# Input sums begun in the chunk's own step, and all four sums of a forward unit at the step's head: one change to a fused spectral mixing and MLP kernel

## The chip, the cores and the metric

The kernel runs on one NeuronCore of a Trainium2 chip. Its time is the device time of one execution in microseconds (us). Five engines work side by side, each through its own queue in order: TensorE (PE in the profile; PEld is its weight loading), VectorE (DVE), ScalarE (ACT), GpSimd (POOL) and SyncE (SP, which here only issues transfers). Transfers are also issued from GpSimd's queue. Sixteen DMA engines carry all of them.

## The reference

```python
def _attn_ref(x, filt_r, filt_i):            # x: (8, 3008, 256), filters: (1505, 256)
    X = np.fft.rfft(x, axis=1)
    F = (filt_r + 1j * filt_i)[None, :, :]
    return np.fft.irfft(X * F, n=x.shape[1], axis=1).astype(np.float32)

def _moe_ref(x, w_in, w_out):                # x: (24064, 256), w_in: (256, 2048), w_out: (2048, 256)
    h = x @ w_in
    relu6 = np.clip(h + 3.0, 0.0, 6.0)
    g = h * relu6 / 6.0
    return (g @ w_out).astype(np.float32)

# reference: _moe_ref(_attn_ref(x, filt_r, filt_i).reshape(24064, 256), w_in, w_out)
```

A sequence is filtered in frequency, and every token then passes an MLP with the activation hard-swish. All is float32.

## The kernel before, in words

**The MLP** works in 47 blocks k of 512 tokens (256 pairs), each in 8 parts p of 256 hidden columns. One (k, p) is a *step*; a plain step takes 6.08 us. "12.3" below is step 3 of block 12. Both products are done by a Strassen scheme with seven products of half size instead of eight. In a step TensorE does seven up products of block k (`up_1` to `up_5`) and seven down products of the step before (`down`), woven together. ScalarE copies partial results (L990, L991, L1000, L1019) and computes the inner part of the activation (L1024). VectorE adds (L1005, L1010), finishes the activation (L1029, in `hswish`) and makes the sums that the down products need (L1036, L1037 in `g_sums`, L1042 in `g_last`). `hswish(1)` and `g_sums` of a step are issued at the beginning of the next one, and its second down product needs them.

**The input sums** of a block, `xt`, are five combinations of the four parts of the block's spectral result (`xn`, a ring of three blocks). They are needed from the next block's first step on (`up_1`). They are made in one of two ways when `ready(i)` finds that chunk i completes a block. For most blocks ScalarE makes five copies (`t_copy`, L956), and three calls of `t_add` (L961) issue transfers from GpSimd's queue that add other parts in place: the first adds to four of the five sums, the second to four beginning with another one, the third is two transfers, of which one adds the tile `minus`. Because they add to the same places, each waits for the landing of the one before. For the other blocks `t_sums` lets GpSimd compute them (L970).

**The spectral part** for the later batches is spread over the MLP's steps. A table `plan` holds for each step five *places* with calls. In a step with a unit the order is: place 3, the activation's rest and `g_sums`, `g_last` unless the step counts as late, place 4, first down products, `up_1`, place 0, more down products, `up_2`, L1005, L1010 and the rest, place 1 (behind `up_4` and the first L1024), `up_5`, the last down products, place 2. Each engine gets its instructions in this order. A step i counts as late (`late`) in steps 1 and 2 of a block, and when places 0 to 2 of step i-1 hold one of the heavy VectorE functions, `a8_sums` among them; then `g_last` follows L1010 instead of `g_sums`.

From batch 2 on the work of batch n follows a cycle of six blocks, named in `kinds` by the letters "caxFFF". The first three (c, a, x) do the forward transform of four chunks c = 0 to 3, and the three F blocks the rest of it, the filter and the inverse transform. A *forward unit* is:

- `a8_unit` (L609, place 3): 32 small matmuls into four PSUM banks, two of which ScalarE copies (L613);
- `a8_sums(n, c, r)` for r = 0 and 1 (L619, L620): a sum and a difference of a copied and a PSUM half, in VectorE;
- `a8_folds(n, c, par)` (L627), two calls one step apart: they write two tiles `y`, of which there are only two buffers;
- `z8_store` (L648 to L654): the tiles go to DRAM, half of the stores from GpSimd's queue and half from SyncE's.

In groups n = 3 to 7 the units stand at steps c.3, a.2, x.2 and x.5, the folds of chunk 2 at x.3 and x.4, its store at the end of x.4, the first fold of chunk 3 at the end of x.5, and its store at the end of x.6. For n = 2 chunk 0 and 1 stand a little later (c.5, a.3). `t2_load` reads the stored values back at the end of block x, for F.2.

The chunk that completes a block does so in step 1 of the block before the one that uses the sums; 30 of these blocks (the a, x and F blocks of six groups) take the way by copies and transfers.

Of the kernel before, what the change touches and what calls it, by code (L numbers as in the profile page):

```python
# [229 lines left out]
def kernel(  # L230
# [585 lines left out]
    for b in range(B):  # L816
# [4 lines left out]
        n = 0  # L821
# [12 lines left out]
    def pair(i):  # L834
        b, js, o, n = chunks[i]
        return b * HC * NA + o, n
# [39 lines left out]
    def ready(i):  # L876
        t, n = pair(i)
        k = t // PAIRS
        if (t + n) // PAIRS > k > 0:
            if n_at[i] % NP == 1 and k - 1 in kinds:  # L880
                st["xt", k] = xtp.tile([P, 5, PAIRS], FP32, name="xt")
                for j, (step, place_) in enumerate(((1, 1), (2, 0), (2, 1), (2, 1), (3, 0), (3, 1), (3, 2), (4, 1))):
                    plan.setdefault((n_at[i] + step, place_), []).append((t_copy if j < 5 else t_add, (k, j % 5)))
            else:
                t_sums(k)


    def n_five(i, ends_step=False):
        b, js, o, n = chunks[i]
        s0 = i % 2 * NJ  # L890
        banks = [psU.tile([P, 512], FP32, name=x) for x in ("al", "be")] if ends_step else [
            psF.tile([P, 512], FP32, name="psn", tag="f") for c in range(2)]
        ps = [t[:, 0:2 * n].rearrange("p (e n) -> p e n", e=2) for t in banks]
        for q, j in enumerate(js):
            for dh in range(2):
                for g in range(2):
                    for c in range(2):
                        r = ds(c * HALF, ATOM)
                        nc.tensor.matmul(ps[c][ts(g, HALF), dh, ts(q, NA)], t4[r, s0 + q, ds(dh * P + g * HALF, HALF)],  # L899
                                         groups[r, j, :], start=True, stop=True)  # L900
        for c in range(2):
            ring(i, 0, n, o, lambda at_: xn[:, :, c, at_], ps[c])
        ready(i)

    def n_unit(i, dh):
        if spare[i]:
            ps = st["po", n_at[i] // NP][2][:, 1, :, :].rearrange("p u m -> p (u m)") if dh else st["al"][:, 256:512]
        else:
            ps = psF.tile([P, 512], FP32, name="psn", tag="f")
        b, js, o, n = chunks[i]  # L910
        for q, j in enumerate(js):
            w = edges[0:2 * ATOM, FIRST.index(j), :] if i >= TAIL and j else ones[0:2 * ATOM, j, :]
            strips(ps[:, ts(q, TOK)], t4[0:2 * ATOM, i % 2 * NJ + q, ts(dh, P)], w, start=not spare[i], stop=True)
        for q, a, m, to in TO.get(i, [(q, 0, NA, o + q * NA) for q in range(len(js))]):
            ring(i, a, m, to, lambda at_: xn[:, dh, :, at_], ps[:, ts(q, TOK)].rearrange("p (c n) -> p c n", c=2))
        if dh:
            ready(i)
# [45 lines left out]
    def t_sums(k):  # L963
        t = xtp.tile([P, 5, PAIRS], FP32, name="xt")
        c0, s0, c1, s1 = (xb(k, d, c) for d in range(2) for c in range(2))
        u, v = (t[:, i, :] for i in (F5, F3))
        f1, f2, f3, f4, f5 = (t[:, i, :] for i in (F1, F2, F3, F4, F5))
        for o, x0, x1, op_ in ((f1, c0, s0, ALU.subtract), (u, c0, c1, ALU.add), (v, s0, s1, ALU.add),
                               (f4, u, v, ALU.subtract), (f5, u, v, ALU.add), (f2, c1, s1, ALU.add), (f3, f1, f2, ALU.add)):
            nc.gpsimd.tensor_tensor(out=o, in0=x0, in1=x1, op=op_)  # L970
        st["xt", k] = t
# [211 lines left out]
    plan = {}  # L1183
# [4 lines left out]
    def at(step, fn, *a):  # L1188
        plan.setdefault((step, 0 if fn in EARLY else 1 if fn is w_scale else 2), []).append((fn, a))

    with tc.manual_schedule():
# [184 lines left out]
        def places(n):  # L1376
            if n == 1:
                return (list(range(2, NB + 2)), [12, 13, 14, 15, 20, 21, 22, 23, 28, 29, 30, 31],
                        [13, 14, 15, 18, 21, 22, 23, 26, 29, 30, 31, 32], [19, 27, 34])
            k = first[n] * NP  # L1380
            each = lambda at_: [k - (4 - r) * NP + s for r in range(3) for s in at_]
            return [k - 7 * NP + i for i in (A2_AT if n == 2 else A_AT)], each((2, 2, 3, 4)), each((3, 4, 5, 5)), each((7,))
# [17 lines left out]
        for n in range(1, B):  # L1400
            a_at, f_at, y_at, bi_at = places(n)
            if n > 1:
                k = (first[n] - 7) * NP
                for i in range(XCUTS):
                    at(k - (47 if n > 2 else 28) + 3 * i // 2, x_twice, n, i)
                for i in range(8):
                    at(k - (33 if n > 2 else 15) + i, x_back, n, i)
            for c, s in enumerate(a_at):
                if n == 1:
                    at(s, a_unit, n, c)  # L1410
                    at(s, a_sums, n, c)
                    at(s, z_store, n, c, nc.sync)
                    if c >= 3:
                        at(max(a_at[c - 3], s - 6), x_load, n, c)
                    continue
                k = (first[n] - 7) * NP
                sums, folds, load = (SUM2_AT, FOLD2_AT, LOAD2_AT) if n == 2 else (SUM_AT, FOLD_AT, LOAD_AT)
                at(s, a8_sums, n, c, 1)
                for d in range(2):
                    at(k + sums[c][d], half_sums, n, c, d)  # L1420
                    at(k + load[c], half_load, n, c, d)
                    at(k + folds[c][d], a8_folds, n, c, d)
                plan.setdefault((s, 3), []).append((a8_unit, (n, c)))
                plan.setdefault((s, 4), []).append((a8_sums, (n, c, 0)))
                zero = (ZERO2_AT if n == 2 else ZERO_AT) if c == 0 else ()
                for j, (r, place_) in enumerate(zero):
                    plan.setdefault((k + r, place_), []).append((a8_zero, (n, j)))
                if zero:
                    plan.setdefault((k + zero[-1][0], 1), []).append((z8_store, (n, c)))
                else:  # L1430
                    at(k + folds[c][1], z8_store, n, c)
            for c in range(NT):
                if n == 1:
                    s = f_at[2 * (c - TB) + 1] + 1 if c >= TB else a_at[-1] + 1
                else:
                    s = a_at[-1] + (2, 2, 5)[c] if c < TB else f_at[(c - TB) // 2 * 4] + 1 + (c == 4)
                at(s, t2_load, n, c)
                s = f_at[2 * (c - FB) + 1] + 1 if c >= FB else a_at[-1] + (1 if n == 1 else (-4, -2)[c])
                at(s, table_load, n, c)
                if n == 2:  # L1440
                    at(s + 3, table_sign, c)
                    at(s + 3, table_store, c)
            for i in range(NU):
                if n == 1:
                    at(f_at[i - i % 2], b_unit, n, i)
                elif i % 4 == 0:
                    plan.setdefault((f_at[i], 3), []).append((b8_unit, (n, i // 4)))
                    plan.setdefault((f_at[i], 4), []).append((f_unit, (n, i)))
                if n == 1 or i % 4:
                    at(f_at[i], f_unit, n, i)  # L1450
                at(y_at[i], y_unit, n, i)
            for r, s in enumerate(bi_at):
                plan.setdefault((s, 3), []).append((bi8_unit, (n, r)))
                plan.setdefault((s, 4), []).append((bi8_sums, (n, r, 0)))
                at(s, bi8_sums, n, r, 1)
                at(s, g8_store, n, r)
# [128 lines left out]
```

## Time and profile before

| | |
|---|---|
| three runs | 2552.65, 2554.51, 2558.05 us, median 2554.51 |
| the profiled execution's own time | 2556.45 us |
| its span (first to last instruction) | 2554.5 us |
| TensorE, VectorE, ScalarE, GpSimd busy | 2535.5, 2011.2, 1370.4, 423.8 us |
| granted TensorE clock | 1.0 |
| accumulating transfers, issue to landing | 2.6 to 12.7 us, middle 5.5 |

The profile is of one execution. An engine's busy time is the union of its instructions' times, without waits and issues of transfers. In lists in order of time a row has start, duration, engine, line, operation, what is written and read, and the number of instructions run together; in brackets stands the idle time before, and what ended it. In the list of waits a row has who waited for whom, the total in us, how often, and the longest. In lists of transfers the last number is the middle time from issue to landing.

### The profile page before, as it was taken

What the parts mean: (1) busy time and instruction counts of PE and PEld (TensorE: products, weight loads), DVE (VectorE), ACT (ScalarE), POOL (GpSimd) and SP (SyncE); (2) the same over time, 40 slices, a digit from 0 to 9 for tenths busy, and PEclk for the clock granted to TensorE, in tenths of its full rate; (3) what the DMA queues carried; (4) which work ended last, traced back from release to release, by engine and by line L of the source; (5) the groups of instructions that cost most, each with busy time, mean ns of one, the idle gap of its engine ahead of it and who ended that gap; (6) DMA issues with size and microseconds to landing.
All of it is one profiled execution on the core that took longest, in us unless ns stands there. A gap on an engine that the chain in (4) does not pass through costs nothing.

```text
span 2554.5 us, 87293 instructions
## 1 busy us (share of the span) xinstructions
PE 2535.5 (99%) x37890; PEld 2002.6 (78%) x37890; DVE 2011.2 (79%) x3645; ACT 1370.4 (54%) x2866; POOL 423.8 (17%) x558
## 2 busy tenths in 40 slices
PE   8999999999999999999999999999999999999999
PEld 4488777777877778777787777877788777888887
DVE  6978888788787787878878788787887778766666
ACT  4554455555555555555555555555555555555554
POOL 3252011111211112111121111211112111011110
PEclk9999999999999999999999999999999999999999
DMA  8845546744455344553445534555433543211000
GB/s 237 237 118 164 169 130 178 176 116 110 117 123 143 84 109 117 127 135 88 116 117 123 134 91 109 124 119 131 104 79 81 114 108 91 62 45 26 19 22 26
DMA packets 222341, 288.70 MB, mean 113 GB/s; under 512 B 23274, under 2 KB 187912, under 8 KB 221574
## 3 DMA queue, kind: packets, MB, share of 16 engines
q1 hardware_dynamic: 163997, 200.76, 27.1%
q0 software_dynamic: 57632, 82.08, 17.2%
q8 instruction: 297, 4.87, 0.8%
q14 instruction: 86, 0.70, 0.1%
q10 hardware_dynamic: 329, 0.30, 0.0%
HBM read 164.38 MB, written 128.81 MB: 115 GB/s over the span
## 4 chain that ended last, share of the span: by engine, by line
PE 95%; DMA 3%; DVE 1%; issue 0%; ACT 0%; SPq 0%; POOL 0%; DVEq 0%; POOLq 0%
PE po L975 45%; PE al L975 25%; PE be L975 18%; PE psn L899 2%; DMA xt<-xn 1%; PE al L780 1%; DMA zp_tmp<-y 1%; PE be L609 1%; PE psf L707 1%; PE psf L694 0%; DMA g_tmp<-t 0%; PE psf L590 0%; DVE y L627 0%; DVE g L1029 0%; PE psf L764 0%
## 5 line engine op out<-in xcount | busy, mean ns | idle before, releaser
L975 PEld LDWEIGHTS po<-w_all,g 128*64 128x64 f32 x20808 | 1237.0, 137 | 272.2 <-issue 35.4
L975 PE MATMUL po<-w_all,g 128*64 128x128 f32 (+1 forms) x20808 | 1418.7, 274 | 0.9 <-DVE g L1029 0.3
L1024 ACT ACTIVATE r<-h,half_c 128x512 f32<-128x512 f32 x736 | 531.1, 722 | 303.7 <-DVE h L1005 291.5
L975 PE MATMUL al<-xt,w_all 128*64 128x256 f32 x4416 | 668.9, 381 | 3.3 <-DMA xt<-xn 3.2
L1029 DVE SCALAR_TENSOR_TENSOR g<-r,h 128x512 f32<-128x512 f32 x736 | 517.8, 704 | 127.6 <-ACT r L1024 118.1
L975 PE MATMUL be<-xt,w_all 128*64 128x256 f32 x2944 | 443.1, 379 | 0.0
L1005 DVE TENSOR_TENSOR h<-be,s 128x512 f32<-128x512 f32 x368 | 253.9, 690 | 201.1 <-PE be L975 168.5
L975 PEld LDWEIGHTS be<-xt,w_all 128*64 128x64 f32 x2944 | 212.2, 137 | 105.5
L1019 ACT ACTIVATE h<-al 128x256 f32<-128x256 f32 x368 | 140.4, 382 | 270.5 <-PE al L975 268.4
L975 PEld LDWEIGHTS al<-xt,w_all 128*64 128x64 f32 x4416 | 273.4, 137 | 11.7 <-issue 3.5
L1010 DVE TENSOR_TENSOR h<-al,s 128x256 f32<-128x256 f32 x368 | 156.0, 424 | 148.0 <-PE al L975 147.9
L1037 DVE TENSOR_TENSOR g<-g 128x512 f32<-128x512 f32 x367 | 255.6, 697 | 12.6
L975 PE MATMUL al<-xn,w_all 128*64 128x256 f32 (+1 forms) x1536 | 240.0, 392 | 1.0 <-DVE g L1029 0.6
L975 PE MATMUL be<-xn,w_all 128*64 128x256 f32 (+1 forms) x1536 | 239.1, 391 | 0.0
L991 ACT ACTIVATE s<-be 128x256 f32<-128x256 f32 x368 | 141.1, 383 | 178.7 <-PE be L975 178.7
L961 POOL DMA_DIRECT2D xt<-xn x90 | 124.6, 1384 | 604.9 <-ACT xt L956 382.0
L1000 ACT ACTIVATE s<-al 128x256 f32<-128x256 f32 x368 | 141.2, 384 | 146.4 <-PE al L975 146.2
L990 ACT ACTIVATE s<-al 128x256 f32<-128x256 f32 x368 | 141.5, 385 | 68.7 <-PE al L975 65.0
L1036 DVE TENSOR_TENSOR g<-g 128x256 f32<-128x256 f32 x367 | 161.8, 441 | 12.6
L975 PEld LDWEIGHTS be<-xn,w_all 128*64 128x64 f32 x1536 | 105.5, 137 | 69.6 <-issue 7.4
L1042 DVE TENSOR_TENSOR g<-g 128x256 f32<-128x256 f32 x367 | 155.1, 423 | 1.7
L970 POOL TENSOR_TENSOR xt<-xn 128x256 f32<-128x256 f32 x64 | 49.5, 791 | 401.9 <-ACT xn L873 401.9
(200 smaller groups left out, 1933.3 us busy)
## 6 DMA issues: line engine op xcount, KB each, us to landing
xt<-xn POOLq DMA_DIRECT2D x60, 512.0 KB, 7.3
g_tmp<-t POOLq DMA_DIRECT2D x96, 256.0 KB, 4.4
x_tmp<-in_x_dram SPq DMA_DIRECT2D x54, 384.0 KB
t<-g_tmp SPq DMA_DIRECT2D x168, 120.0 KB
ft<-f_tmp SPq DMA_DIRECT2D x36, 512.0 KB
t<-zp_tmp SPq DMA_DIRECT2D x36, 512.0 KB
o_tmp<-o SPq DMA_DIRECT2D x46, 256.0 KB
zp_tmp<-y POOLq DMA_DIRECT2D x96, 96.0 KB, 4.9
```

Of the source, the lines that this page charges most:

```text
L975: nc.tensor.matmul(ps[ds(o, STRIP)], w[:, ds(o, STRIP)], x, skip_group_check=True, **kw)
L990: nc.scalar.activation(out=s[:, 0, :], in_=al, func=AXT.Copy)
L991: nc.scalar.activation(out=s5, in_=be[:, 1, :], func=AXT.Copy)
L1000: nc.scalar.activation(out=s[:, 1, :], in_=al, func=AXT.Copy)
L1005: nc.vector.tensor_tensor(out=st["h"][0].rearrange("p (a n) -> p a n", a=2), in0=be, in1=s, op=ALU.add)
L1010: nc.vector.tensor_tensor(out=st["h"][1][:, 256:512], in0=al, in1=s5, op=ALU.add)
L1019: nc.scalar.activation(out=st["h"][1][:, 0:256], in_=al, func=AXT.Copy)
L1024: nc.scalar.activation(out=r, in_=st["h"][i], func=AXT.Relu, bias=half_c, scale=1.0 / 6.0)
L1029: nc.vector.scalar_tensor_tensor(out=st["g", k, p][:, o:o + 2, :].rearrange("p a n -> p (a n)"), in0=st["r", i], scalar=1.0, in1=st["h"][i ...
L1036: v.tensor_tensor(out=g[:, G1, :], in0=g[:, G3, :], in1=g[:, G22, :], op=ALU.add)
L1037: v.tensor_tensor(out=g[:, G3:G2 + 1:2, :], in0=g[:, G3:G1 + 1, :], in1=g[:, G11:G11 + 1, :].broadcast_to([P, 2, 256]), op=ALU.subtract)
L1042: nc.vector.tensor_tensor(out=g[:, G4, :], in0=g[:, G12, :], in1=g[:, G2, :], op=ALU.subtract)
```

## The change

The calls of `t_copy` and `t_add` get earlier places. The five copies stood one to three steps behind the chunk's own step; the first two now stand in place 1 of the chunk's own step, the next two in place 1 of the step behind it, and the last in place 0 of the second step behind it. The three adds stood at the third step behind (places 1 and 2) and the fourth (place 1); now they stand at place 2 of the first step behind and at places 1 and 2 of the second.

Both calls of `a8_sums` now stand in place 4. Before, the second (the index 1) stood in place 2 of the same step.

```diff
@@ -879,7 +879,7 @@ ready
-                for j, (step, place_) in enumerate(((1, 1), (2, 0), (2, 1), (2, 1), (3, 0), (3, 1), (3, 2), (4, 1))):
+                for j, (step, place_) in enumerate(((0, 1), (0, 1), (1, 1), (1, 1), (2, 0), (1, 2), (2, 1), (2, 2))):
                     plan.setdefault((n_at[i] + step, place_), []).append((t_copy if j < 5 else t_add, (k, j % 5)))
@@ -1415,13 +1415,12 @@
-                at(s, a8_sums, n, c, 1)
                 for d in range(2):
                     at(k + sums[c][d], half_sums, n, c, d)
                     at(k + load[c], half_load, n, c, d)
                     at(k + folds[c][d], a8_folds, n, c, d)
                 plan.setdefault((s, 3), []).append((a8_unit, (n, c)))
-                plan.setdefault((s, 4), []).append((a8_sums, (n, c, 0)))
+                plan.setdefault((s, 4), []).extend([(a8_sums, (n, c, 0)), (a8_sums, (n, c, 1))])
```

## The prediction

> **What bounds the kernel now.** I read the page first, then the list of waits, then the order in time of VectorE and GpSimd around one block.
>
> ```profile
> PE 2535.5 (99%) x37890; PEld 2002.6 (78%) x37890; DVE 2011.2 (79%) x3645; ACT 1370.4 (54%) x2866; POOL 423.8 (17%) x558
> PE 95%; DMA 3%; DVE 1%; issue 0%; ACT 0%; SPq 0%; POOL 0%; DVEq 0%; POOLq 0%
> ```
>
> TensorE is busy for 2535.5 of 2554.5 us. A change that adds no matmuls can win at most the 19 us between, and can lose any amount if it makes TensorE wait. The chain of work shows the same: 95% TensorE, 3% transfers. The list of waits says which transfers:
>
> ```profile
> POOL xt L961 <- DMA xt<-xn: 90.7, 15, 9.0
> POOL zp_tmp L648 <- DVE y L627: 68.2, 13, 6.2
> PE al L975 <- DMA xt<-xn: 3.2, 3, 1.6
> ```
>
> The second transfer of the sums waits on GpSimd's queue until the first has landed (first line), GpSimd's z stores wait for VectorE's folds (second), and TensorE lost only 3.2 us to late sums (third).
>
> The place that decides is block 12, step 2 to step 6 (731 to 763 us), an x block in the kinds "caxFFF". GpSimd in order of time, with its idle time and what ended it in brackets:
>
> ```profile
> 741.65 1.30 POOL L961 DMA_DIRECT2D xt<-xn  x1 [15.37 <-issue]
> 748.92 2.07 POOL L648 DMA_DIRECT2D zp_tmp<-y  x4 [5.97 <-DVE y L627]
> 754.19 1.33 POOL L961 DMA_DIRECT2D xt<-xn  x1 [3.20 <-ACT s L1000]
> 762.86 0.88 POOL L961 DMA_DIRECT2D xt<-minus  x1 [7.34 <-DMA xt<-xn]
> 763.42 1.54 POOL L961 DMA_DIRECT2D xt<-xn  x1
> 764.14 2.90 POOL L648 DMA_DIRECT2D zp_tmp<-y  x4
> ```
>
> The order is first add, four z stores of chunk 2, second add, the third add (two transfers), z stores of chunk 3. The transfers' own times from issue to landing, from the list of issues in windows around 742, 754 and 764 us:
>
> ```profile
> xt<-xn POOLq DMA_DIRECT2D x1, 512.0 KB, 10.8
> xt<-xn POOLq DMA_DIRECT2D x1, 512.0 KB, 8.1
> zp_tmp<-y POOLq DMA_DIRECT2D x4, 96.0 KB, 7.9
> ```
>
> VectorE at the same place:
>
> ```profile
> 750.93 0.68 DVE L619 TENSOR_TENSOR t<-t,psf 128x512 f32<-128x512 f32 x1
> 751.65 0.69 DVE L620 TENSOR_TENSOR t<-t,psf 128x512 f32<-128x512 f32 x1
> 753.64 0.69 DVE L1005 TENSOR_TENSOR h<-be,s 128x512 f32<-128x512 f32 x1 [1.31 <-PE be L975]
> ...
> 755.74 0.68 DVE L619 TENSOR_TENSOR t<-t,psf 128x512 f32<-128x512 f32 x1
> 756.45 0.69 DVE L620 TENSOR_TENSOR t<-t,psf 128x512 f32<-128x512 f32 x1
> 757.05 1.28 DVE L627 TENSOR_TENSOR y<-t 128x512 f32<-128x512 f32 x2
> 758.26 0.69 DVE L1029 SCALAR_TENSOR_TENSOR g<-r,h 128x512 f32<-128x512 f32 x1
> ```
>
> The reader is to see three things: 1.31 us of idle time at the head of the step, the second pair of sums at its end (755.74), and behind it the first fold of chunk 3 (757.05). That fold writes the y buffer whose contents GpSimd's four stores of chunk 2 are carrying away; they landed at 755.6, so it just didn't wait.
>
> **The change part by part.**
>
> *Four sums at the head.* Nothing is added; 24 times (six groups of four chunks) two VectorE operations move from the step's end to its head. A pair occupies 1.32 us (736.09 to 737.41 in block 12; 0.71 + 0.61). They go into the 1.31 us that VectorE waits for TensorE before L1005. In 23 steps the gap is 1.28 us or more, so L1005 is 0.04 us late at most; in one (434.64 us) it is 0.92, so 0.40. L1010 and TensorE's last up product follow L1005 closely there (that product's matmul x4 takes 0.65 instead of 0.60 already), so I count these delays in full: 0.4 + 23 x 0.02 = about 1 us. Bounds: 0, and 24 x 0.40 = 9.6. At the end of the step VectorE is 1.32 us freer. In three of four groups the next step lasts its 6.08 us with TensorE full, so nothing comes of it; in the fourth (x step 6) the next step is 0.34 us too long (6.42 instead of 6.08 between the starts of TensorE's `be<-xn` products; 0.55 in block 6), 2.3 us in all, because folds and sums together make L1029 late. That would be won, if the folds could begin at once. In 17 steps the fourth product sum (L1042, 0.42 us) also moves to the head, since the rule for late steps no longer counts this sum; L1029 there starts 0.27 us earlier and L1005 waits for TensorE anyhow. Cost 0; without that cover 17 x 0.33 = 5.6.
>
> *ScalarE's copies one step earlier.* 30 blocks, five copies each, 0.41 us (0.61 for the first). In step 1 they fall behind L1024; ScalarE is idle 1.09 us there before L1019 and the two take about 0.95. In step 2 two of 0.41 take the place of one of 0.61. Cost 0; without cover some 0.3 us x 30 = 9.
>
> *Accumulating transfers earlier in GpSimd's queue.* Four transfers per block. Blocks where the sums now come late gain: the steps that start blocks 7, 13, 25 and 31 are 0.49, 1.54, 1.75 and 0.19 us over-long, 4.0 us in all, the bulk of which is the 3.2 us above. In a and F blocks nothing behind them is urgent: the a block's z stores of chunk 1 have until the x block's step 3, and the F blocks' last sums land 0.9 to 10 us before the block ends already. In the x blocks the order in the queue turns over: all adds (steps 2 and 3) now stand before the z stores of chunk 2 (end of step 4). A queue that waits for a landing holds what is behind it. For block 12:
> - The copy that the first add needs runs at 740.70 now and at about 735.35 then; the add starts 0.95 us behind it, at 736.3.
> - It lands after d0. In the six x blocks d0 is 7.7, 10.8, 11.2, 11.8, 12.0 and 11.7 us; in F blocks from 5.4. The row of its own block is nearest, since the transfers that it meets (705 KB out, two tables of 512 KB, the reordered input; DMA share 0.85 in 737 to 743 and 1.02 in 743 to 751) start at 735.6 and it still meets them. I take 10.0: landed at 746.3.
> - 0.6 to the next issue (0.57 to 2.17), then d1: 11.5, 8.1, 7.7, 7.5, 7.9, 5.5 in x blocks. I take 8.0: landed at 754.9.
> - 0.6 again: the third add starts at 755.5. From its start to the landing of the z stores issued behind it the six blocks show 9.3 to 11.7; chunk 3's other stores aren't there to share now, so 9.0: landed at 764.5.
>
> VectorE reaches the fold at 755.7 and stands until 764.5. L1029 then starts at 765.7 instead of 758.26. TensorE's second down product needs its result and already waits about 0.3 us for it today, so each microsecond is one of TensorE: 7.4, and 0.2 for L1010, which the next up product needs. Block 12 thus loses 7.6 us, and all six x blocks have this order: 45.6 us. The six steps' 2.3 us are not won then.
>
> [...]
>
> **Sum.** The profiled execution took 2556.45 us (span 2554.5), 1.9 above the median of 2554.51. +45.6 (x blocks) - 4.0 (late sums) + 1.0 (head) = +42.6. That gives 2599.0 for an execution like the profiled one and 2597 against the median.
>
> Bounds of the large term: with the fastest rows everywhere (5.4 + 0.6 + 5.5 + 0.6, then 3.3 to the last store's issue and 2.1, its fastest landing) the stores have landed at 753.8, and nothing waits; then 4.0 and 2.3 are won. With the slowest (12.0 + 2.2 + 11.5 + 0.6 + 11.7) the fold waits until 774.3 and each block loses some 17 us, 104 in all.
>
> **The rivals.**
>
> *The queue keeps up* (faster). If no x block's stores are late, the change wins 4.0 + 2.3 and pays 1.0: 2549. It decides where both large adds together take less than about 10 us, so that with the 1.2 and 9.0 us behind them the stores have landed by 756.7. F blocks come near (5.4 and 6.0); no x block does (17.2 at least). Chance 0.07.
>
> *It nearly keeps up.* Stalls of 1 to 5 us per x block, because the first add, 5 us earlier, meets less traffic: for it speaks the DMA share of 0.08 up to 736.9 us; against it that the 705 KB begin at 735.6. At 2 us it is 12 - 3 = +9: 2563. At the low end (1 us) it is +3, within the measurement. Chance 0.13, 0.04 of it no difference.
>
> *The stall slows what follows.* TensorE was never idle for more than 1.6 us after its start, and the page's clock row shows 9 tenths or more in all forty slices. If after 7 us of standing it came back at half pace for the first half of a 6.08 us step, each x block would pay 3.0 us more: 18 us, 2615. Nothing in this trace can show it. [...] Chance 0.15.
>
> *Stalls as computed*: 5 to 11 us per block, 2582 to 2618. Chance 0.65.
>
> **How the numbers follow.** The forecast is 2597. The range leaves out the first rival and the lower half of the second (about 0.13) and the upper tail of the third (0.06): 2566 to 2620. A difference under 0.2% (5 us) can't be told from none here. Faster 0.07, same 0.04, slower 0.89.
>
> **What would show it.** In the profile after, GpSimd should show first add, second add, third add and then z stores in each x block, with the first add near x step 2 + 4.8 us. VectorE's wait for y (L627) on zp_tmp should appear with six entries near 8 us, and TensorE's wait for L1029 with six near 7. The waits for xt should be gone from TensorE, and the 24 heads should show L1005 without idle time before it. The forecast is wrong if the two large adds together need less than 13 us in x blocks, or if something else gives VectorE work that doesn't depend on that fold.

## The result and the profile after

| | before | after |
|---|---|---|
| median of six runs each, us | 2554.93 | 2614.73 |
| their range | 2552.65 to 2558.05 | 2613.14 to 2616.13 |
| the profiled execution's own time | 2556.45 | 2615.83 |
| its span | 2554.5 | 2613.7 |
| TensorE, VectorE, GpSimd busy | 2535.5, 2011.2, 423.8 | 2550.2, 2015.8, 423.0 |
| mean granted TensorE clock | 1.0 | 0.99 |

The kernel became slower, by a ratio of 1.0233 [1.022, 1.0247]; between the medians lie 59.8 us, between the two profiled executions 59.4. The forecast was +42.6, that is 2597 in a range from 2566 to 2620.

Of the page, the busy times and the chain that ended last (after):

```profile
PE 2550.2 (98%) x37890; PEld 2013.6 (77%) x37890; DVE 2015.8 (77%) x3645; ACT 1370.6 (52%) x2866; POOL 423.0 (16%) x558
PE 94%; DMA 3%; DVE 1%; POOL 1%; SPq 0%; issue 0%; ACT 0%; DVEq 0%; POOLq 0%
```

The reader is to see that TensorE is busy for 14.7 us more than before with the same 37890 matmuls. Work was not added, so the same work ran slower somewhere. The rest of the 59.4 us is idle time. The list of waits (after) has it; its columns are who waited for whom, total us, how often, the longest:

```profile
POOL zp_tmp L648 <- DVE y L627: 65.7, 7, 11.1
DVE y L627 <- DMA zp_tmp<-y: 54.2, 6, 10.1
PE po L975 <- DVE g L1029: 47.6, 6, 9.0
```

VectorE's wait of its fold (L627) for the z stores wasn't in the list before at all; it comes six times, once in each x block, and TensorE's wait for VectorE's L1029 comes six times with it. TensorE's wait for late sums (3.2 us before) is gone.

GpSimd in block 12, from step 2 to step 7 (after; start, duration, instruction, idle time before it and what ended that):

```profile
746.98 1.36 POOL L961 DMA_DIRECT2D xt<-xn  x1 [10.05 <-issue]
757.63 1.29 POOL L961 DMA_DIRECT2D xt<-xn  x1 [9.30 <-ACT r L1024]
769.79 0.87 POOL L961 DMA_DIRECT2D xt<-minus  x1 [10.86 <-ACT s L1000]
770.35 1.53 POOL L961 DMA_DIRECT2D xt<-xn  x1
771.07 2.87 POOL L648 DMA_DIRECT2D zp_tmp<-y  x4
```

All three adds now stand before the four z stores of chunk 2. The stores were ready when VectorE had folded, but they were issued only when the second add had landed, at 771.07. VectorE at the same place:

```profile
763.62 0.69 DVE L620 TENSOR_TENSOR t<-t,psf 128x512 f32<-128x512 f32 x1
764.29 0.69 DVE L1005 TENSOR_TENSOR h<-be,s 128x512 f32<-128x512 f32 x1
...
776.58 1.29 DVE L627 TENSOR_TENSOR y<-t 128x512 f32<-128x512 f32 x2 [10.12 <-DMA zp_tmp<-y]
777.79 0.69 DVE L1029 SCALAR_TENSOR_TENSOR g<-r,h 128x512 f32<-128x512 f32 x1
```

It comes to the fold of chunk 3 at 766.46 and starts it at 776.58. Behind it, L1029 is late by the same, and TensorE (in order of time, after):

```profile
768.92 0.60 PE L975 MATMUL be<-xt,w_all 128*64 128x256 f32 x4
778.53 1.98 PE L975 MATMUL po<-w_all,g 128*64 128x128 f32 x16 [9.01 <-DVE g L1029]
780.29 1.07 PE L975 MATMUL al<-xt,w_all 128*64 128x256 f32 x4
...
783.65 1.04 PE L975 MATMUL po<-w_all,g 128*64 128x128 f32 x16
784.52 0.60 PE L975 MATMUL al<-xt,w_all 128*64 128x256 f32 x4
```

The sixteen matmuls of a down product take 1.98 us at 778.53 and 1.04 at 783.65; four of an up product 1.07 and then 0.60. The busy times by windows (after; the number behind the five engines is the granted clock) say why:

```profile
770.00:772.00 2.00, 0.00 (x0) 0.00 (x0) 0.00 (x0) 0.00 (x0) 2.00 (x4) 1.00 0.48 79
772.00:774.00 2.00, 0.00 (x0) 0.00 (x0) 0.00 (x0) 0.00 (x0) 1.94 (x4) 0.83 0.92 132
774.00:776.00 2.00, 0.00 (x0) 0.00 (x0) 0.00 (x0) 0.00 (x0) 0.00 (x0) 0.50 0.75 199
...
783.00:784.00 1.00, 1.00 (x14) 0.68 (x12) 0.97 (x2) 0.14 (x1) 0.34 (x1) 0.71 0.00 0
784.00:786.00 2.00, 2.00 (x30) 1.55 (x28) 0.93 (x2) 1.35 (x3) 1.62 (x4) 1.00 0.50 107
```

The clock falls to half at about 773.3, while TensorE stands (0.83 of the window to 774), and comes back at about 783.6 (0.71 of the window to 784). TensorE works again from 778.5, so 5.1 us of its work went at half pace. In the six x blocks together the trace has 29.7 us of work at half clock; half of that, 14.9, is about the 14.7 by which TensorE was busy longer.

**Where the difference lies.** Step x.6 is step 6 of an x block. Step lengths are taken from one start of TensorE's `be<-xn` product to the next; a plain one is 6.08 us. The rows add up to 59.2, the difference of the two spans.

| part | before | after | difference |
|---|---|---|---|
| the six steps x.6, above 6.08 each | 2.24 | 63.32 | +61.1 |
| first steps of blocks 7, 13, 25, 31, above 6.08 each | 3.95 | 0 | -4.0 |
| all other steps | | | +0.6 |
| before the first step of block 1 | 125.15 | 126.65 | +1.5 |

The last row belongs to the single execution: it was between 122.9 and 127.5 in the runs told below. Within the six steps x.6 TensorE's idle time went from 0.9 to 47.6 us, the six waits, and its busy time rose by 14.5; together that is the 61.1.

### The profile page after: what moved, and what is told of

It reads as the page before. It is cut to its first block, busy times and chain, and to the rows that moved or that the text cites. A ratio compares the mean times of both kernels' runs of the same rounds, so it can differ in the third digit from the quotient of the medians.

```text
span 2613.7 us, 87345 instructions
## 1 busy us (share of the span) xinstructions
PE 2550.2 (98%) x37890; PEld 2013.6 (77%) x37890; DVE 2015.8 (77%) x3645; ACT 1370.6 (52%) x2866; POOL 423.0 (16%) x558
## 4 chain that ended last, share of the span: by engine, by line
PE 94%; DMA 3%; DVE 1%; POOL 1%; SPq 0%; issue 0%; ACT 0%; DVEq 0%; POOLq 0%
PE po L975 44%; PE al L975 25%; PE be L975 18%; PE psn L899 2%; DMA zp_tmp<-y 1%; PE be L609 1%; PE al L780 1%; PE psf L707 1%; DMA bits<-in_moe_w_in_dram 0%; PE psf L694 0%; POOL xt L961 0%; DMA t<-g_tmp 0%; PE psf L590 0%; DMA w_all<-in_x_dram 0%; DMA xb_tmp<-in_x_dram 0%
## 5 line engine op out<-in xcount | busy, mean ns | idle before, releaser
L975 PE MATMUL po<-w_all,g 128*64 128x128 f32 (+1 forms) x20808 | 1429.4, 276 | 47.6 <-DVE g L1029 47.6
L1029 DVE SCALAR_TENSOR_TENSOR g<-r,h 128x512 f32<-128x512 f32 x736 | 518.3, 704 | 151.6 <-ACT r L1024 142.7
L1005 DVE TENSOR_TENSOR h<-be,s 128x512 f32<-128x512 f32 x368 | 253.8, 690 | 168.0 <-PE be L975 134.7
L1042 DVE TENSOR_TENSOR g<-g 128x256 f32<-128x256 f32 x367 | 155.4, 423 | 2.3
L1133 POOL TENSOR_TENSOR o<-p,o 128x256 f32<-128x256 f32 x45 | 33.0, 734 | 510.9 <-DVE o L1131 384.5
```

The source lines that it names most:

```text
L975: nc.tensor.matmul(ps[ds(o, STRIP)], w[:, ds(o, STRIP)], x, skip_group_check=True, **kw)
L1005: nc.vector.tensor_tensor(out=st["h"][0].rearrange("p (a n) -> p a n", a=2), in0=be, in1=s, op=ALU.add)
L1029: nc.vector.scalar_tensor_tensor(out=st["g", k, p][:, o:o + 2, :].rearrange("p a n -> p (a n)"), in0=st["r", i], scalar=1.0, in1=st["h"][i ...
L1042: nc.vector.tensor_tensor(out=g[:, G4, :], in0=g[:, G12, :], in1=g[:, G2, :], op=ALU.subtract)
```

## The experiments

Theory A, that of the forecast: the z stores of chunk 2 stand behind adds that wait for landings, and VectorE's fold waits for them. Theory B adds to it that TensorE comes back from these waits at half pace. Rivals to A: the four sums at the head delay the step; the adds and copies, being earlier, disturb the blocks elsewhere; the transfers merely share the DMA engines, whatever their order.

**One part alone: the sums at the head.**

```diff
 # after, with the old places of copies and adds
-  enumerate(((0, 1), (0, 1), (1, 1), (1, 1), (2, 0), (1, 2), (2, 1), (2, 2)))
+  enumerate(((1, 1), (2, 0), (2, 1), (2, 1), (3, 0), (3, 1), (3, 2), (4, 1)))
```

> Only the second part of the change: both calls of the sums at the head of a forward unit, copies and adds at their old places. Theory (the whole loss comes from GpSimd's queue order in the x blocks): 2552 to 2555 us, since the six steps x.6 that are 0.34 to 0.55 us too long become plain and nothing else changes; L1005 without idle time at the 24 heads. Rival (the four sums at the head hold up VectorE and TensorE): 2565 or more.

Measured: 2552.21 us (2551.32 to 2558.06, ten runs), ratio 0.9988 [0.9978, 0.9997]. The slowness isn't in this part; it may even win a little (0.03 to 0.22%). The steps x.6 went from 2.24 us above plain to 2.15 only: four of them became plain or nearly so, but that of block 24 is now 1.40 too long and that of block 6 is 0.68, and the trace says why. VectorE in order of time, around 1391 us:

```profile
1391.52 0.69 DVE L627 TENSOR_TENSOR y<-t 128x512 f32<-128x512 f32 x1 [0.81 <-DMA zp_tmp<-y]
...
1393.60 0.69 DVE L627 TENSOR_TENSOR y<-t 128x512 f32<-128x512 f32 x1 [1.39 <-DMA zp_tmp<-y]
```

With the sums out of the way the folds come earlier, and now wait for the z stores themselves, up to 1.4 us. (The fold's first instruction writes the tile that GpSimd's queue stores, the second the one that SyncE's queue stores.) So already the order of before had hardly more than a microsecond to spare there.

**The other part alone: copies and adds earlier.**

```diff
 # before, with the new places of copies and adds; a8_sums as before
-  enumerate(((1, 1), (2, 0), (2, 1), (2, 1), (3, 0), (3, 1), (3, 2), (4, 1)))
+  enumerate(((0, 1), (0, 1), (1, 1), (1, 1), (2, 0), (1, 2), (2, 1), (2, 2)))
```

> Only the first part: copies and adds early, the second pair of sums at the step's end as before. Theory: the end of the wait is set by the landing of the z stores, so the second pair of sums is hidden in it: 2613 to 2617 us, six waits of VectorE for zp_tmp, each about 1.3 us shorter than the 8.2 to 10.1 of the changed kernel. Rival (both parts are needed, or the sums at the head carry part of the loss): 2560 to 2600.

Measured: 2614.35 us (2612.55 to 2616.78), ratio 1.0227 [1.0209, 1.0246]: the whole loss, within the interval. From its list of waits:

```profile
PE po L975 <- DVE g L1029: 49.0, 6, 9.9
DVE y L627 <- DMA zp_tmp<-y: 47.8, 6, 9.7
```

VectorE stands 6.4 us less than with both parts (47.8 against 54.2); in this kernel it still makes the second pair of sums, 1.3 us, before each of the six folds. TensorE stands about the same (49.0, 47.6), since what counts is when the stores land.

**Only the order in the queue, by other means.** Nothing of the change is in this kernel: chunk 2's stores are put one step later, and so behind the third add at its old place.

```diff
 # before
-                    at(k + folds[c][1], z8_store, n, c)
+                    at(k + folds[c][1] + (c == 2), z8_store, n, c)
```

> The kernel before, with one thing changed: the z stores of chunk 2 (GpSimd's and SyncE's halves) are issued one step later, at the end of step x.5, and so stand behind the third add, whose place is the old one. No copy, add or sum moves. Theory (the order in GpSimd's queue is the cause, and early adds only soften it): the stores start behind the third add, in block 12 near 764 instead of 749 us, and land near 773; the fold waits some 16 us instead of 9, TensorE loses that and 2.5 to 4 us at half clock, six times: 2640 to 2670 us. Rival (early adds and what they meet on the DMA engines are needed for the loss): below 2600.

Measured: 2626.22 us (2624.09 to 2629.95), ratio 1.028 [1.0263, 1.0298]; the direction is as expected, the size is below. In block 12 (GpSimd in order of time) the queue has the order of after:

```profile
753.27 1.30 POOL L961 DMA_DIRECT2D xt<-xn  x1 [15.37 <-issue]
764.73 1.27 POOL L961 DMA_DIRECT2D xt<-xn  x1 [10.16 <-ACT s L991]
774.01 0.88 POOL L961 DMA_DIRECT2D xt<-minus  x1 [8.01 <-issue]
774.58 1.54 POOL L961 DMA_DIRECT2D xt<-xn  x1
775.28 2.89 POOL L648 DMA_DIRECT2D zp_tmp<-y  x4
```

and the waits answer to it:

```profile
PE po L975 <- DVE g L1029: 63.1, 6, 12.3
DVE y L627 <- DMA zp_tmp<-y: 61.8, 6, 12.0
```

So the order alone, with every add where it always was, makes the same two waits and the same kind of loss. (SyncE's half of these stores moves with GpSimd's here; the 12.0 us stand before the fold's first tile, which is GpSimd's.) The expectation was too high mostly because I had put in 9 us from the stores' issue to the fold; in all six blocks it took 5.2 to 5.6. The second add took 5.5 to 9.7 us.

**Take away what the fold waits for: another pair of tiles for chunk 3.** Two more buffers for `y` don't fit: a later pool needs 8 KB per partition, and 0.59 KB would be left. So chunk 3 borrows the tiles of the half sums.

```diff
 # after; QU - 1 is chunk 3
-            st["cs", b, m] = [yp.tile([P, 2, 2, D], FP32, name="y") for i in range(2)]
+            two = (t1p, "t1") if m == QU - 1 else (yp, "y")
+            st["cs", b, m] = [two[0].tile([P, 2, 2, D], FP32, name=two[1]) for i in range(2)]
```

> The changed kernel, with the folded tiles of chunk 3 in another pair of buffers (those of the half sums, which stand free there): the order in GpSimd's queue and all transfers stay, and only what makes the fold wait is taken away. Theory: VectorE's wait for zp_tmp (54.2 us) and TensorE's wait behind it (47.6 us) go, the clock stays at 1.00, and the gains stay (late sums 4.0, steps x.6 2.3): 2547 to 2552 us. Rival (the early adds crowd the DMA engines, and something else is late then): 2565 or more, with a new wait on a transfer in the x blocks.

Measured: 2551.61 us (2549.14 to 2552.72, eleven runs), ratio 0.9983 [0.9974, 0.9991]. Two lists of the trace in order of time, GpSimd and VectorE in block 12 (all lines from 626 on are one further down here):

```profile
746.83 1.29 POOL L962 DMA_DIRECT2D xt<-xn  x1 [11.19 <-ACT h L1020]
758.64 0.87 POOL L962 DMA_DIRECT2D xt<-minus  x1 [10.52 <-ACT r L1025]
759.21 1.53 POOL L962 DMA_DIRECT2D xt<-xn  x1
759.93 2.88 POOL L649 DMA_DIRECT2D zp_tmp<-y  x4
```

```profile
753.07 0.69 DVE L1030 SCALAR_TENSOR_TENSOR g<-r,h 128x512 f32<-128x512 f32 x1
753.68 1.28 DVE L628 TENSOR_TENSOR t<-t 128x512 f32<-128x512 f32 x2
754.88 0.68 DVE L1030 SCALAR_TENSOR_TENSOR g<-r,h 128x512 f32<-128x512 f32 x1
```

GpSimd's order is that of after and chunk 2's stores leave as late (759.93, behind the third add), yet the fold at 753.68 has no idle time before it, since it writes `t1` tiles. VectorE's wait for `zp_tmp` is gone from the list of waits, all six steps x.6 are plain, the mean granted clock is 0.999 (0.99 in after), and TensorE is busy for 2533.4 us (2550.2 in after). That settles that the loss is this wait and what follows from it, and not the earlier adds, the copies or the traffic as such. By the medians this kernel is 63.1 us (2614.73 to 2551.61) faster than after, and it also beats before, by 0.09 to 0.26%. The late sums at the heads of four blocks and the over-long x.6 are both won in it.

**Old places in the x blocks only.** `OLD` and `NEW` stand for the two lists of places in the first two experiments.

```diff
 # after
-  enumerate(NEW)
+  enumerate(OLD if kinds[k - 1] == "x" else NEW)
```

> The changed kernel, but in the x blocks the copies and adds have their old places; a and F blocks keep the early ones. Theory: the loss goes entirely, the steps x.6 are plain, and the late sums of blocks 7, 13, 25 and 31 stay, since x blocks make them: 2551 to 2555 us. Rival (early adds in a and F blocks cost as well, by crowding): 2558 or more.

Measured: 2554.39 us (2550.58 to 2559.57, ten runs), ratio 1.0001 [0.9992, 1.001]. The whole loss comes from the x blocks. Nothing is won either: two late sums (1.13 and 0.87 us) remain, and

```profile
DVE y L627 <- DMA zp_tmp<-y: 4.6, 9, 0.9
```

are the small waits of the first experiment again.

**One add or two of the x blocks behind the z stores.** The first of the two kernels puts the third add behind the stores, the second also the second. Only the last three places of the list are shown.

```diff
 # after, in the x blocks only
-  (1, 2), (2, 1), (2, 2)
+  (1, 2), (2, 1), (4, 1)      # third add behind
+  (1, 2), (3, 2), (4, 1)      # second and third behind
```

> The changed kernel, but in the x blocks the third add stands at its old place behind the z stores of chunk 2; the first and second stay ahead of them. Theory: the stores are then held only until the first add has landed and the second is issued, about 4 us past their time, and share the engines with the second: VectorE waits 0 to 3 us per block, 2550 to 2565 us in all. Rival (any early add in the x blocks costs the whole stall): 2600 or more.

Measured: 2578.67 us (2577.93 to 2580.37), ratio 1.0095 [1.0082, 1.0109]: some 14 us above the top of what I had expected. GpSimd in block 12, and the fold in VectorE:

```profile
751.21 1.30 POOL L961 DMA_DIRECT2D xt<-xn  x1 [9.33 <-ACT r L1024]
753.12 1.10 POOL L648 DMA_DIRECT2D zp_tmp<-y  x2 [0.61 <-DVE y L627]
755.15 1.01 POOL L648 DMA_DIRECT2D zp_tmp<-y  x2 [0.93 <-issue]
```

```profile
763.89 1.46 DVE L627 TENSOR_TENSOR y<-t 128x512 f32<-128x512 f32 x2 [3.86 <-DMA zp_tmp<-y]
```

The stores aren't held back for a landing here. They are issued as soon as VectorE is done, just behind the second add, and the fold still has to wait until 763.89, some 8.7 us behind the last issue. So a transfer of 512 KB that was issued before them in the same queue is enough. The single packets in the traces of before and after show how such stores follow an add on their queue: the adds move packets of 1 KB, these stores packets of 4 KB. In after, block 12, the issues of the stores begin at 771.07, and their first 4 KB packet starts at 774.04, when 369 of the third add's 384 packets have ended. In before, block 12, where the first add is under way when the stores are issued, their first packet starts at 750.11, when 438 of that add's 512 have ended, while 111 packets of 4 KB of SyncE's queue ended between the add's first packet (743.61) and then. How much of the 8.7 us the sharing with other transfers added stays open. In block 6 alone it was the fold's second tile, SyncE's half, that came last, 5.07 of the 26.0 us that VectorE waits in all.

> The changed kernel, but in the x blocks the second and third add stand behind the z stores of chunk 2 (end of step x.4, step x.5); the first stays early. Theory: the stores start when their folds are done, no wait of VectorE over 1 us for them, and the sums land before the next block starts: 2548 to 2552 us, the best order. Rival (the first add, early, meets the stores' traffic): 2555 or more.

Measured: 2555.34 us (2550.7 to 2557.39, eleven runs), ratio 1.0 [0.9991, 1.0009]. With only the first add ahead of the stores the large loss is gone, as theory A has it, but the expected gain of 3 to 7 us isn't there. The late sums are gone; in exchange

```profile
DVE y L627 <- DMA zp_tmp<-y: 7.4, 8, 2.5
```

and the steps x.6 are 5.31 us above plain (2.24 before), 4.03 of it in one block, where TensorE stood 2.14 us; what made up the rest of the 4.03 is not shown. There the fold waited longest (2.46 us) for its second tile, which SyncE's queue stores; so this part isn't the order in GpSimd's queue, and what held SyncE's stores there is not shown.

**Fill TensorE's wait.** Seven matmuls whose result nobody uses stand before the down product that waits, in the step x.6 of the six x blocks. If TensorE's slowness behind the wait is due to its standing, it should go.

```diff
 # after, behind up_2 and ahead of the second down product
+            if up and p == 6 and kinds.get(k) == "x":
+                ps = psF.tile([P, 512], FP32, name="psf", tag="f")
+                for j in range(7):
+                    nc.tensor.matmul(ps, ...)      # 128x128 by 128x512
```

> The changed kernel with seven matmuls of 128x512 on constant weights ahead of the down products that wait in step x.6 (their result is used by nothing): TensorE works through most of its wait instead of standing. Theory with the clock as a part of the loss: the granted clock stays at 1.00 through the x blocks, the waits end when they did, and the 14 to 15 us that TensorE is busy longer than before go: 2598 to 2603 us. Rival (the clock falls for another reason, or its fall costs nothing because VectorE sets the pace then): 2612 to 2618.

Measured: 2603.62 us (2601.22 to 2605.18), ratio 1.0182 [1.016, 1.0203]: 11.1 us less than after, by adding work. From TensorE in order of time in block 12, and from the waits:

```profile
767.95 6.28 PE L1521 MATMUL psf<-w_all 128*128 128x512 f32 x14
...
777.01 1.21 PE L975 MATMUL po<-w_all,g 128*64 128x128 f32 x16 [2.78 <-DVE g L1029]
```

```profile
DVE y L627 <- DMA zp_tmp<-y: 57.7, 6, 10.3
PE po L975 <- DVE g L1029: 13.9, 6, 3.0
```

and of the page:

```profile
PE 2573.5 (99%) x37974; PEld 2017.5 (78%) x37974; DVE 2015.5 (77%) x3645; ACT 1371.7 (53%) x2866; POOL 422.7 (16%) x558
```

The seven matmuls are fourteen instructions in the trace and take 6.28 us. VectorE stands as long as without them, even 3.5 us longer in all (57.7 against 54.2). But TensorE stands 3.0 us at most, the down product behind it takes 1.21 us instead of 1.98, and the mean granted clock is 0.999 instead of 0.99; in block 12 it still falls (0.59 in the mean from 778 to 782). TensorE's busy time is 2573.5, that is 38.0 more than before, and six times 6.28 are 37.7: the 14.7 us by which the kernel after was busy longer are gone but for 0.3. The time lies 0.6 us above the expected 2603. Theory B holds.

**How long TensorE stood, and the granted clock,** by kernel. The waits are TensorE's for VectorE's L1029 in the lists of waits, the clock is the mean of the profiled execution, the busy time that of the page:

| kernel | TensorE's waits: total us, how often, the longest | mean granted clock | TensorE busy, us |
|---|---|---|---|
| before | 0.3, 1, 0.3 | 1.0 | 2535.5 |
| wait filled | 13.9, 6, 3.0 | 0.999 | 2573.5, of which 37.7 are the added matmuls |
| second and third add behind | 3.2, 2, 2.1 | 0.999 | 2535.3 |
| third add behind | 19.7, 6, 5.0 | 0.996 | 2542.5 |
| after | 47.6, 6, 9.0 | 0.99 | 2550.2 |
| stores one step later | 63.1, 6, 12.3 | 0.988 | 2546.5 |

In the trace of after the clock goes to half once at each of the six waits: for 6.83 us at those of 7.10, 7.29 and 7.29 us, and for 10.24 us at those of 7.88, 9.01 and 9.01. Behind shorter waits in block 12 it falls too: in wait filled, behind 2.78 us, it is 0.59 from 778 to 782, and in third add behind 0.70 from 766 to 768 and 0.50 from 768 to 770. What sets how long it stays at half is not shown.

## Why the prediction was right, and where it fell short

The direction, the place and the mechanism were right, and the time lies in the range; the point was 17.7 us too low. By the prediction's steps, with block 12 for the sizes:

- *Order in GpSimd's queue turns over in the x blocks.* Right: adds one to three, then the stores, and the experiment on the order alone makes the same loss without the change.
- *The first add starts at x.2 + 4.8 us and VectorE reaches the fold 19.4 us later.* Right: 746.98 and 766.46, 19.5 us.
- *The chain of landings, 28.2 us from the first add's start to the fold.* It took 29.6 (776.58). Its terms were off in both directions: the first add 10.1 (taken 10.0), the second 10.5 (8.0), the gap behind it 1.7 (0.6), and from the third add's start to the fold 6.8 (9.0). In the six x blocks the first add took 10.9 in the mean and the second 9.1, and yet the fold waited 9.0 (8.8), because the last term was 6.8 in five of them and 8.7 in one. So the sum was good because errors in its terms cancelled.
- *Each microsecond of VectorE's is one of TensorE's, 7.6 a block.* Right: 47.6 us in six waits, 7.9 a block.
- *Late sums, -4.0.* Right: 3.95 to 0.
- *The sums at the head, +1.0.* Too high. L1005 comes 2.71 us behind the first sum, as before; only in the one place with less cover 2.64 instead of 2.32, and that step is 0.27 longer. So it cost 0.3. Together with what the end of the step wins, the part alone gave 0.9988 of before.
- *Copies and L1042, 0.* Nothing in the list of steps speaks against it: all other steps together are 0.6 us longer.
- *Sum +42.6.* This is the step that failed: it has no term for TensorE's clock. The third rival had the mechanism, at 3.0 us a block and 2615 in all, and I gave it 0.15 because "Nothing in this trace can show it." It measured 14.7 us of longer busy time, 2.45 a block. With it the sum is 57.3, and 59.3 with the 2.0 more of the waits (47.6 against 45.6). Without the 0.7 of the head that weren't paid it is 58.6; the two profiled executions lie 59.4 apart, 1.5 of which stand before block 1 and belong to the single execution. The rival's own 3.0 was an estimate, half of a plain step; the half-clock time with TensorE at work was 5.1 us in block 12, which costs half of that, 2.55.
- *The first rival's limit, 756.7.* A slip: by the prediction's own times the fold is reached at 755.7, so the two large adds would have had to take less than some 9.2 us together, not 10. It decides nothing, since they took 18.5 or more in every x block.

The half pace of the third rival is there in the trace of after at all six waits: 6.83 or 10.24 us at half clock each time, of which TensorE works for 3.8 to 6.0. The trace of before has no such spell between the first and the last matmul.

The rival of the queue that keeps up is ruled out: in the x blocks of after the 512 KB adds took 10.1 to 12.0 us for the first and 7.1 to 10.5 for the second.

## What to carry to other kernels

When a transfer that waits for a landing is moved forward in an in-order queue, look for what stands behind it, find the engine that reuses the buffer which that leaves from, and add up the landings to that engine's next use; here the order in one queue in six blocks cost 59 us, and other buffers for one pair of tiles gave all of it back. When the sum makes TensorE stand for several microseconds, put in a second term for the work that follows at half clock: about 2.5 us for each of the six waits of 7 to 9 us here (14.7 in all). A part that only makes an engine earlier is worth nothing if the next thing that it needs is a store which lands about then.

## What was not expected of the hardware

- What the half clock cost didn't grow with the wait: with the waits of stores one step later, 63.1 us in all and 12.3 at the longest, TensorE's busy time rose by 11.0 (2535.5 to 2546.5), with those of after, 47.6 and 9.0, by 14.7. Part of each spell falls into the wait itself: in after 21.5 of 51.2 us at half clock.
- Matmuls without use, 6.3 us of them in each of six blocks, made the kernel 11.1 us faster.
- The clock fell also behind a wait of TensorE's of only 2.78 us (wait filled, block 12: 0.59 from 778 to 782).
- Four stores of 96 KB, issued as soon as they could be but behind an accumulating transfer of 512 KB on the same queue, let the fold start only 8.7 us behind the last issue in block 12; in after, where these stores stand behind the third add, their first packet started when 369 of its 384 had ended (block 12).
